# Fused block attention and FFN: second chunk's keys from a tile already loaded, later weight loads, later summaries and values

## The chip, the cores and the metric

One core of a Trainium2 chip. The metric is the device time of one execution in microseconds; the median of three runs of the kernel before is 690.5 us (688.78 to 691.71).

## The reference

Four batches, 8 heads, 768 positions, 64 elements per head. Each position attends to the positions less than 16 away and to 24 block summaries of its head, one for each block of 32 positions (the maximum of the block's keys, the mean of its values). The attention output, 3072 tokens of 512, goes through a feed-forward part:

```
scores_l = scale * q @ k^T                      # masked to |i - j| < 16
scores_s = scale * q @ k_sum^T + log(32)        # k_sum: maximum of 32 keys
a        = softmax(concat(scores_l, scores_s))
x        = a @ concat(v, v_sum)                 # v_sum: mean of 32 values
h        = x @ w_in                             # 512 -> 2048
out      = (h * tanh(softplus(h))) @ w_out      # 2048 -> 512
```

The weights arrive as 64-bit floats and are turned into float32 on the chip.

## The kernel before

The tokens are cut into 12 chunks of 256 (3 per batch). A unit is one chunk and one pair of heads; there are 48, and each is worked in phases:

- `att_scores` (L273): 16 matmuls of a 64-query tile against 96 keys and the 24 summaries (L284), or, for chunk 0, 32 matmuls with keys and summaries apart (L288, L290). DVE adds the mask and takes the row extreme (L299), ACT the exponentials (L304).
- `att_normalize` (L309): reciprocals on DVE (L313, L314), the product on POOL (L315).
- `att_transpose` (L317): four PE transposes (L321), one ACT copy to `pt` (L323).
- `att_values` (L326): 16 matmuls (L339), an ACT cast to `xh` (L340), and, by the returned function, the remainder `xl` on DVE (L341).

Two chunks make a group of 512 tokens, on which the feed-forward part (FFN below) runs in 16 steps, one for each block of 128 of the 2048: `ff_in` (12 matmuls, L353), Mish on ACT (L360), a split into two parts (L369, L371), and two steps later `ff_out` (12 matmuls, L381).

**Weights.** `load_weight` (L114) issues 1 MB as two DMAs (L119) into one of two buffers, `begin_weight` (L136) and `join_weight` (L149) make the float32 (ACT L143, DVE L144, L145, L154, L156), `upper_weight` (ACT, L129) and `lower_weight` (DVE, L134) split it. A load waits for the join of the load two before it. The one buffer of `f` makes L143 wait for the L134 before it.

**Order.** Under `tc.manual_schedule()` (L401) each engine runs its instructions in the order written; SP issues all DMAs, one after another, and a DMA that has to wait holds up those behind it. Before the FFN come ten turns u (L416); turn u holds the scores of unit u (u < 8), the values of unit u - 2 and the transposition of unit u - 1. Units 0 to 3 are chunk 0: their keys (`ks`, 768 positions), queries and values are loaded at the start by `first_keys` (L201) and `first_values` (L210), and their value summaries are 16 matmuls (L230, in two halves of 8), an ACT copy (L233) and a DMA from that into the values' tile (L234) in `first_value_summary`. Units 4 to 7 are chunk 1; `att_load_keys` (L244) loads queries and keys in one DMA of 496 KB (L251) and has POOL copy in the key summaries (L252). `att_load_values` (L255) loads `vw` (L258) and copies in the summaries (L259).

The FFN loop (L449) runs over steps i of all six groups; `at` (L396) says in which step which later unit has its scores: steps 0, 2, 4, 6, 8, 10, 12 and 13 in the first group. Transpositions come at the end of the next step, values in step i + 2. In even steps `att_load_keys` also loads `vsum` (L199) for a new batch, in odd ones `att_summaries` reduces it (L240, L241), moves it (L242) and loads the next keys (L195).

**PSUM.** Pool `ps_w` has four buffers, taken in turn by `ph` of `ff_in`, the two tiles of a unit's scores and, in the FFN loop, by `pt_ps` and `x_ps`.

Of the kernel before, what the change touches and what calls it, by code (L numbers as in the profile page):

```python
# [9 lines left out]
F32 = mybir.dt.float32  # L10
# [7 lines left out]
B, H, S, D = 4, 8, 768, 64  # L18
DM, DFF = 512, 2048
BLK, WIN = 32, 16  # L20
P = 128
NB = S // BLK
QT = 64
# [33 lines left out]
def fused_kernel(ctx: ExitStack, tc: tile.TileContext, q0, qk, kt, v0, vw, vs, w_in, w_out, out):  # L57
# [56 lines left out]
    def load_weight():  # L114
        if weights:
            w, fc = weights.pop(0)
            t = stage.tile([P, WB, WP], I64, tag="stage", name=f"w{w}_{fc}")
            for k in range(WB):
                nc.sync.dma_start(t[:, k, :], (w_in, w_out)[w][fc + k])  # L119
            loaded.append((w, fc, t))  # L120
# [28 lines left out]
    def join_weight():  # L149

        if begun:
            w, fc, f, x = begun.pop(0)
            u = f.bitcast(U32)
            nc.vector.tensor_scalar(out=f, in0=f, scalar1=-_as_f32(F32_MAX), scalar2=_as_f32(F32_MAX),  # L154
                                    op0=ALU.max, op1=ALU.min)
            nc.vector.scalar_tensor_tensor(out=u, in0=u, scalar=3, in1=x,  # L156
                                           op0=ALU.logical_shift_left, op1=ALU.bitwise_or)
            joined.append((w, fc, f))
            load_weight()


    begin = ExitStack()
# [23 lines left out]
    summary = {}  # L186
    xs = {}
    units = {}


    sources = {}

    def load_key_source(b, hp):
        ks = sources[b, hp, 0] = stage.tile([P, S], F32, tag="sum", name=f"ks{b}_{hp}", bufs=1)
        nc.sync.dma_start(ks, kt[b, hp])  # L195
# [5 lines left out]
    def first_keys(hp):  # L201

        ks = first_att.tile([P, WIN + S], F32, tag="ks", name=f"ks0_{hp}")
        nc.gpsimd.memset(ks[:, 0:WIN], 0.0)
        nc.sync.dma_start(ks[:, WIN:], kt[0, hp])
        t = first_att.tile([P, CH], F32, tag="q0", name=f"q0_{hp}")
        nc.sync.dma_start(t, q0[hp])
        units[0, hp] = {"q": t, "k": ks}

    def first_values(hp):  # L210
        vwt = first_att.tile([KA, NQ, P], F32, tag="vw", name=f"vw0_{hp}")
        nc.sync.dma_start(vwt[0:KW], vw[0, hp].rearrange("p (s k) -> p s k", s=NQ))
        t = first_att.tile([P, NR, P], F32, tag="v0", name=f"v0_{hp}", bufs=HP)
        nc.sync.dma_start(t, v0[hp].rearrange("p (j d) -> p j d", d=P))
        units[0, hp].update(v=vwt, rest=t)

    def key_summary(b, hp, keys):

# [4 lines left out]
    def first_value_summary(hp):  # L223

        vm = att.tile([KA, P], F32, tag="vm", name=f"vm0_{hp}", bufs=HP)[KW:KA]
        summary[0, hp].append(vm)
        vwt, t = units[0, hp]["v"], units[0, hp]["rest"]
        ps = att_psum(0, f"vm_ps0_{hp}")
        for j in range(NQ + NR):
            nc.tensor.matmul(ps[KW:KA, 0:P], *((blocks[0:KW, j, :], vwt[0:KW, j, :]) if j < NQ else  # L230
                                               (blocks[:, j, :], t[:, j - NQ, :])),
                             start=(j == 0), stop=(j == NQ + NR - 1))
        nc.scalar.copy(vm, ps[KW:KA, 0:P])  # L233
        nc.sync.dma_start(vwt[KW:KA], vm.unsqueeze(1).broadcast_to([NB, NQ, P]))  # L234
# [20 lines left out]
    def att_load_values(c, hp):  # L255
        b = c // CPB
        vwt = att.tile([KA, NQ, P], F32, tag="vw", name=f"vw{c}_{hp}")
        nc.sync.dma_start(vwt[0:KW], vw[c, hp].rearrange("p (s k) -> p s k", s=NQ))  # L258
        nc.sync.dma_start(vwt[KW:KA], summary[b, hp][1].unsqueeze(1).broadcast_to([NB, NQ, P]))  # L259
        units[c, hp]["v"] = vwt  # L260
# [12 lines left out]
    def att_scores(c, hp):  # L273
        u = units[c, hp]
        th = c % CPB


        ps = [att_psum(c, f"sc{c}_{hp}_{h}", scores=True) for h in range(2)]
        for s in range(NQ):
            for h in range(2):  # L280
                r = slice(h * D, (h + 1) * D)
                row, at0 = slice(s % 2 * QT, (s % 2 + 1) * QT), s // 2 * KA
                if c > 0:
                    nc.tensor.matmul(ps[h][row, at0:at0 + KA], u["qk"][r, s, h * QT:(h + 1) * QT],  # L284
                                     u["qk"][r, s, P:], start=True, stop=True)
                    continue
                q = u["q"][r, s * QT:(s + 1) * QT]
                nc.tensor.matmul(ps[h][row, at0:at0 + KW], q, u["k"][r, s * QT:s * QT + KW],  # L288
                                 start=True, stop=True)
                nc.tensor.matmul(ps[h][row, at0 + KW:at0 + KA], q, summary[0, hp][0][r, :],  # L290
                                 start=True, stop=True)
        pr = (att if c else first_att).tile([P, NQ, KA], F32, tag="pr", name=f"pr{c}_{hp}")


        nm = small.tile([P, NQ], F32, tag="nm", name=f"nm{c}_{hp}")
        for j in range(NQ):
            h, pair = divmod(j, NQ // 2)
            m = first if th == 0 and pair == 0 else last if th == CPB - 1 and pair == NQ // 2 - 1 else base
            nc.vector.tensor_tensor_reduce(  # L299
                out=pr[:, j, :], in0=ps[h][:, pair * KA:(pair + 1) * KA], in1=m, scale=-SCALE,  # L300
                scalar=-NEG, op0=ALU.add, op1=ALU.min, accum_out=nm[:, j:j + 1])
        sm = small.tile([P, NQ], F32, tag="sm", name=f"sm{c}_{hp}")
        for s in range(NQ):
            nc.scalar.activation(pr[:, s, :], pr[:, s, :], AF.Exp, scale=-1.0, bias=nm[:, s:s + 1],  # L304
                                 accum_out=sm[:, s:s + 1])
        u["p"] = pr
        u["sm"] = sm
# [9 lines left out]
    def att_transpose(c, hp):  # L317
        u = units[c, hp]
        ps = att_psum(c, f"pt_ps{c}_{hp}")
        for s in range(NQ):  # L320
            nc.tensor.transpose(ps[:KA, s * P:(s + 1) * P], u["p"][:, s, :], ident)  # L321
        pt = att.tile([KA, NQ, P], F32, tag="pt", name=f"pt{c}_{hp}", bufs=1)
        nc.scalar.copy(pt.rearrange("p s q -> p (s q)"), ps[:KA, :])  # L323
        u["pt"] = pt
# [91 lines left out]
    for u in range(n + 2):  # L416
        if u % 2 == 0:
            upper_weight()
        if u < n:
            att_scores(*todo[u])  # L420
        if u < HP:
            first_value_summary(u)
        lower = att_values(*todo[u - 2]) if 2 <= u else None
        if u % 2:
            join_weight()
        else:
            lower_weight()
            begin_weight()
        if u + 1 < HP:
            key_summary(0, u + 1, units[todo[u + 1]]["k"][:, WIN:])  # L430
        if lower:
            lower()
        if u == HP + 1:
            begin.close()
            late += weight_tiles(ctx.enter_context(tc.tile_pool(name="late", bufs=1)), "w_late", NFC - EARLY)
        if u < n:
            att_normalize(*todo[u])
        if HP - 2 <= u < n:
            att_load_keys(*todo[u + 2])
        if HP <= u:  # L440
            att_load_values(*todo[u])
        if 1 <= u <= n:
            att_transpose(*todo[u - 1])

    load_key_source(1, 0)
    waiting = []
    for i in range(len(steps) + 2):  # L449
        upper_weight()  # L450
        if i < len(steps):
            ff_in(*steps[i])
            ff_act(*steps[i])
            if i < NFC:
                waiting.append(ff_split(*steps[i]))
        if 0 < i <= NFC:
            waiting.pop(0)()
        lower_weight()
        lower = att_values(*at[i - 2]) if i - 2 in at else None
        if lower and i >= NFC:  # L460
            lower()
        if i in at:
            att_scores(*at[i])
        begin_weight()
        if lower and i < NFC:
            lower()
        if NFC <= i < len(steps):
            ff_split(*steps[i])()
        if i in at:
            att_normalize(*at[i])  # L470
        join_weight()
        if i in at:
            if todo.index(at[i]) + 2 < len(todo):
                att_load_keys(*todo[todo.index(at[i]) + 2])
        if i - 2 in at and todo.index(at[i - 2]) + 2 < len(todo):
            att_load_values(*todo[todo.index(at[i - 2]) + 2])
        if i - 1 in at:
            att_summaries(todo.index(at[i - 1]) + 2)
        if i >= 2:
            ff_out(*steps[i - 2])  # L480
        if i - 1 in at:
            att_transpose(*at[i - 1])
# [44 lines left out]
```

## Time and profile before

| what | value |
|---|---|
| median of three runs | 690.5 us |
| profiled execution | 691.24 us, of which the span is 689.5 us |
| PE busy | 641.1 us (93%) |
| DVE busy | 290.6 us (42%) |
| ACT busy | 332.9 us (48%) |
| POOL busy | 68.1 us (10%) |
| moved by DMA | 71.05 MB |
| mean granted TensorE clock | 0.967 |

PE is the tensor engine's matmuls, DVE the vector engine, ACT the scalar engine, POOL GpSimd and SP the engine that issues DMAs. Shares over the whole span hide that its stretches differ: the turns before the FFN, the first FFN steps with weights still being prepared, and the rest. A bracket in a timeline row is the engine's idle time just before the instruction, with what released it.

### The profile page before, as it was taken

What the parts mean: (1) busy time and instruction counts of PE and PEld (TensorE: products, weight loads), DVE (VectorE), ACT (ScalarE), POOL (GpSimd) and SP (SyncE); (2) the same over time, 40 slices, a digit from 0 to 9 for tenths busy, and PEclk for the clock granted to TensorE, in tenths of its full rate; (3) what the DMA queues carried; (4) which work ended last, traced back from release to release, by engine and by line L of the source; (5) the groups of instructions that cost most, each with busy time, mean ns of one, the idle gap of its engine ahead of it and who ended that gap; (6) DMA issues with size and microseconds to landing.
All of it is one profiled execution on the core that took longest, in us unless ns stands there. A gap on an engine that the chain in (4) does not pass through costs nothing.

```text
span 689.5 us, 10881 instructions
## 1 busy us (share of the span) xinstructions
PE 641.1 (93%) x4160; PEld 513.9 (75%) x4160; DVE 290.6 (42%) x836; ACT 332.9 (48%) x722; POOL 68.1 (10%) x119
## 2 busy tenths in 40 slices
PE   4845798879999999999999999999999999999997
PEld 3634576667778878878878878878788788888886
DVE  3866889895223225453232244442242232221112
ACT  2655776668555445454554554454464454111111
POOL 3121011021101001001001001001001000000000
PEclk9866899999999999999999999999999999999999
DMA  8776455744232122542112134432141110010001
GB/s 281 197 259 217 153 190 212 213 152 141 59 106 87 45 67 92 158 153 89 45 48 85 44 130 114 134 113 68 45 140 54 45 59 0 1 62 0 1 1 61
DMA packets 31253, 71.05 MB, mean 103 GB/s; under 512 B 4833, under 2 KB 9953, under 8 KB 31201
## 3 DMA queue, kind: packets, MB, share of 16 engines
q1 hardware_dynamic: 31200, 70.35, 31.9%
q8 instruction: 33, 0.54, 0.3%
q14 instruction: 20, 0.16, 0.1%
HBM read 61.54 MB, written 6.29 MB: 98 GB/s over the span
## 4 chain that ended last, share of the span: by engine, by line
PE 79%; DMA 6%; ACT 6%; DVE 5%; issue 2%; SPq 1%; POOL 0%; POOLq 0%; ACTq 0%; DVEq 0%
PE po L381 35%; PE ph L353 34%; PE x_ps L339 4%; PE sc L284 3%; PE pt_ps L321 3%; DVE w_f L156 2%; DMA vsum<-vs 2%; DMA q<-q 1%; DMA v<-v 1%; DVE w_f L154 1%; ACT w_f L143 1%; DMA qk<-qk 1%; ACT pr L304 1%; DMA vw<-vm 1%; ACT L360 1%
## 5 line engine op out<-in xcount | busy, mean ns | idle before, releaser
L360 ACT ACTIVATE a<-ph 128x512 f32<-128x512 f32 x96 | 57.4, 598 | 155.4 <-PE ph L353 155.0
L369 DVE CAST ah<-a 128x512 fp32r<-128x512 f32 x80 | 34.0, 425 | 197.1 <-ACT a L360 197.1
L353 PE MATMUL ph<-xh,w_early_in_hi 128*128 128x512 f32 x240 | 97.8, 407 | 0.0
L381 PE MATMUL po<-w_early_out_hi,ah 128*128 128x512 f32 x240 | 97.5, 406 | 0.0
L360 ACT ACT_TABLE_LOAD x41 | 52.6, 1283 | 88.6 <-PE ph L353 88.4
L353 PE MATMUL ph<-xh,w_early_in_lo 128*128 128x512 f32 x240 | 94.9, 396 | 0.0
L353 PE MATMUL ph<-xl,w_early_in_hi 128*128 128x512 f32 x240 | 94.8, 395 | 0.0
L381 PE MATMUL po<-w_early_out_lo,ah 128*128 128x512 f32 x240 | 94.3, 393 | 0.0
L381 PE MATMUL po<-w_early_out_hi,al 128*128 128x512 f32 x240 | 94.1, 392 | 0.0
L315 POOL TENSOR_TENSOR pr<-pr,rs 128x480 f32<-128x480 f32 x48 | 49.2, 1026 | 394.9 <-DVE rs L314 327.5
L304 ACT ACTIVATE pr<-pr,nm 128x120 f32<-128x120 f32 x192 | 73.5, 384 | 16.8 <-DVE nm L299 16.3
L341 DVE TENSOR_TENSOR xl<-x_ps,xh 128x256 fp32r<-128x256 f32 x48 | 20.3, 423 | 119.8 <-ACT xh L340 119.8
L371 DVE TENSOR_TENSOR al<-a,ah 128x512 fp32r<-128x512 f32 x96 | 66.3, 691 | 2.8
L381 PE MATMUL po<-w_late_out_hi,ah 128*128 128x512 f32 x144 | 58.0, 403 | 0.0
L353 PE MATMUL ph<-xh,w_late_in_hi 128*128 128x512 f32 x144 | 57.6, 400 | 0.0
L381 PE MATMUL po<-w_late_out_lo,ah 128*128 128x512 f32 x144 | 56.3, 391 | 0.0
L353 PE MATMUL ph<-xh,w_late_in_lo 128*128 128x512 f32 x144 | 56.2, 391 | 0.0
L353 PE MATMUL ph<-xl,w_late_in_hi 128*128 128x512 f32 x144 | 56.1, 390 | 0.0
L381 PE MATMUL po<-w_late_out_hi,al 128*128 128x512 f32 x144 | 56.0, 389 | 0.0
L381 PEld LDWEIGHTS po<-w_early_out_hi,ah 128*128 128x128 f32 x240 | 45.7, 190 | 13.1 <-issue 4.4
L339 PEld LDWEIGHTS x_ps<-pt,vw 120*64 120x64 f32 x768 | 29.0, 149 | 33.5 <-issue 18.5
L353 PEld LDWEIGHTS ph<-xh,w_early_in_lo 128*128 128x128 f32 x240 | 45.8, 191 | 10.2
(74 smaller groups left out, 934.5 us busy)
## 6 DMA issues: line engine op xcount, KB each, us to landing
qk<-qk SPq DMA_DIRECT2D x44, 496.0 KB
vw<-vw SPq DMA_DIRECT2D x48, 192.0 KB
w<-w_in SPq DMA_DIRECT2D x16, 512.0 KB
w<-w_out SPq DMA_DIRECT2D x16, 512.0 KB
ks<-kt SPq DMA_DIRECT2D x17, 384.0 KB
out<-o SPq DMA_DIRECT2D x24, 256.0 KB
vsum<-vs SPq DMA_DIRECT2D x12, 384.0 KB
vw<-vm SPq DMA_DIRECT2D x48, 48.0 KB
```

Source lines behind the costliest of these rows:

```text
L156: nc.vector.scalar_tensor_tensor(out=u, in0=u, scalar=3, in1=x, op0=ALU.logical_shift_left, op1=ALU.bitwise_or)
L284: nc.tensor.matmul(ps[h][row, at0:at0 + KA], u["qk"][r, s, h * QT:(h + 1) * QT], u["qk"][r, s, P:], start=True, stop=True)
L304: nc.scalar.activation(pr[:, s, :], pr[:, s, :], AF.Exp, scale=-1.0, bias=nm[:, s:s + 1], accum_out=sm[:, s:s + 1])
L315: nc.gpsimd.tensor_mul(pr, pr, rs.unsqueeze(2).broadcast_to([P, NQ, KA]))
L321: nc.tensor.transpose(ps[:KA, s * P:(s + 1) * P], u["p"][:, s, :], ident)
L339: nc.tensor.matmul(x, u["v"][:, s, d], pt, start=True, stop=True)
L341: return lambda: nc.vector.tensor_sub(xl, ps[:, :CH], xh.bitcast(F32))
L353: nc.tensor.matmul(ph, w[:, cc * P:(cc + 1) * P], x[:, cc, :], start=(cc == 0 and n == 0), stop=(cc == NCC - 1 and n == 2))
L360: nc.scalar.activation(a, st[g, fc], AF.Mish)
L369: (nc.scalar.copy if g == 0 else nc.vector.tensor_copy)(ah, a)
L371: return lambda: nc.vector.tensor_sub(al, a, ah.bitcast(F32))
L381: nc.tensor.matmul(po[g][t], a[:, tok], w, start=(fc == 0 and n == 0), stop=(fc == NFC - 1 and n == 2))
```

## The change

Five edits. Chunk 1 takes its keys from `ks`, shifted by 256 positions, and its scores are the 32 matmuls of chunk 0; the queries' tile is twice as wide, and `more_queries` fills the second half with two DMAs per unit in turns 2 to 5, from the part of `qk` that holds queries (4 runs of 64 floats in each of 64 partitions per DMA). The tile of values `v0` is kept in `rests`. The pool of the first turns is closed in turn 7, not 5. The weights' load is the last thing in an odd turn, and in an FFN step comes after the loads of keys, values and summaries. The value summaries of units 0 to 3 come behind the transposition. The values of units whose scores are in steps 0 to 10 come three steps later, not two.

```diff
--- before.py
+++ after.py
@@ -156,7 +156,6 @@
             nc.vector.scalar_tensor_tensor(out=u, in0=u, scalar=3, in1=x,
                                            op0=ALU.logical_shift_left, op1=ALU.bitwise_or)
             joined.append((w, fc, f))
-            load_weight()
 
 
     begin = ExitStack()
@@ -186,6 +185,7 @@
     summary = {}
     xs = {}
     units = {}
+    rests = {}
 
 
     sources = {}
@@ -203,16 +203,25 @@
         ks = first_att.tile([P, WIN + S], F32, tag="ks", name=f"ks0_{hp}")
         nc.gpsimd.memset(ks[:, 0:WIN], 0.0)
         nc.sync.dma_start(ks[:, WIN:], kt[0, hp])
-        t = first_att.tile([P, CH], F32, tag="q0", name=f"q0_{hp}")
-        nc.sync.dma_start(t, q0[hp])
-        units[0, hp] = {"q": t, "k": ks}
+        t = first_att.tile([P, CG * CH], F32, tag="q0", name=f"q0_{hp}")
+        nc.sync.dma_start(t[:, :CH], q0[hp])
+        for c in range(CG):
+            units[c, hp] = {"q": t[:, c * CH:(c + 1) * CH], "k": ks[:, c * CH:]}
+
+    def more_queries(hp):
+
+        t, other = units[1, hp]["q"], qk[1, hp].rearrange("p (s k) -> p s k", s=NQ)
+        for h in range(2):
+            r = slice(h * D, (h + 1) * D)
+            nc.sync.dma_start(t[r].rearrange("p (s k) -> p s k", s=NQ), other[r, :, h * QT:(h + 1) * QT])
 
     def first_values(hp):
         vwt = first_att.tile([KA, NQ, P], F32, tag="vw", name=f"vw0_{hp}")
         nc.sync.dma_start(vwt[0:KW], vw[0, hp].rearrange("p (s k) -> p s k", s=NQ))
         t = first_att.tile([P, NR, P], F32, tag="v0", name=f"v0_{hp}", bufs=HP)
         nc.sync.dma_start(t, v0[hp].rearrange("p (j d) -> p j d", d=P))
-        units[0, hp].update(v=vwt, rest=t)
+        units[0, hp].update(v=vwt)
+        rests[hp] = t
 
     def key_summary(b, hp, keys):
 
@@ -224,7 +233,7 @@
 
         vm = att.tile([KA, P], F32, tag="vm", name=f"vm0_{hp}", bufs=HP)[KW:KA]
         summary[0, hp].append(vm)
-        vwt, t = units[0, hp]["v"], units[0, hp]["rest"]
+        vwt, t = units[0, hp]["v"], rests.pop(hp)
         ps = att_psum(0, f"vm_ps0_{hp}")
         for j in range(NQ + NR):
             nc.tensor.matmul(ps[KW:KA, 0:P], *((blocks[0:KW, j, :], vwt[0:KW, j, :]) if j < NQ else
@@ -280,7 +289,7 @@
             for h in range(2):
                 r = slice(h * D, (h + 1) * D)
                 row, at0 = slice(s % 2 * QT, (s % 2 + 1) * QT), s // 2 * KA
-                if c > 0:
+                if c >= CG:
                     nc.tensor.matmul(ps[h][row, at0:at0 + KA], u["qk"][r, s, h * QT:(h + 1) * QT],
                                      u["qk"][r, s, P:], start=True, stop=True)
                     continue
@@ -418,8 +427,6 @@
             upper_weight()
         if u < n:
             att_scores(*todo[u])
-        if u < HP:
-            first_value_summary(u)
         lower = att_values(*todo[u - 2]) if 2 <= u else None
         if u % 2:
             join_weight()
@@ -430,20 +437,27 @@
             key_summary(0, u + 1, units[todo[u + 1]]["k"][:, WIN:])
         if lower:
             lower()
-        if u == HP + 1:
+        if u == n - 1:
             begin.close()
             late += weight_tiles(ctx.enter_context(tc.tile_pool(name="late", bufs=1)), "w_late", NFC - EARLY)
         if u < n:
             att_normalize(*todo[u])
-        if HP - 2 <= u < n:
+        if HP - 2 <= u < n - 2:
+            more_queries(u + 2 - HP)
+        if n - 2 <= u < n:
             att_load_keys(*todo[u + 2])
         if HP <= u:
             att_load_values(*todo[u])
         if 1 <= u <= n:
             att_transpose(*todo[u - 1])
-
-
-
+        if u < HP:
+            first_value_summary(u)
+        if u % 2:
+            load_weight()
+
+
+
+    values = {i + (3 if i < NFC - 4 else 2): unit for i, unit in at.items()}
     load_key_source(1, 0)
     waiting = []
     for i in range(len(steps) + 2):
@@ -456,7 +470,7 @@
         if 0 < i <= NFC:
             waiting.pop(0)()
         lower_weight()
-        lower = att_values(*at[i - 2]) if i - 2 in at else None
+        lower = att_values(*values[i]) if i in values else None
         if lower and i >= NFC:
             lower()
         if i in at:
@@ -472,10 +486,11 @@
         if i in at:
             if todo.index(at[i]) + 2 < len(todo):
                 att_load_keys(*todo[todo.index(at[i]) + 2])
-        if i - 2 in at and todo.index(at[i - 2]) + 2 < len(todo):
-            att_load_values(*todo[todo.index(at[i - 2]) + 2])
+        if i in values and todo.index(values[i]) + 2 < len(todo):
+            att_load_values(*todo[todo.index(values[i]) + 2])
         if i - 1 in at:
             att_summaries(todo.index(at[i - 1]) + 2)
+        load_weight()
         if i >= 2:
             ff_out(*steps[i - 2])
         if i - 1 in at:
```

## Rows read from the trace of the kernel before

**Rows 1.** Three stretches: length, busy us of each engine (instructions), PEclk, DMA share, GB/s.

```profile
0.00:62.00 62.00, 32.73 (x416) 24.93 (x416) 39.20 (x115) 30.66 (x93) 14.62 (x41) 0.79 0.75 239
62.00:160.00 98.00, 82.66 (x482) 64.87 (x481) 81.42 (x143) 69.17 (x121) 10.81 (x11) 0.91 0.56 186
160.00:689.50 529.50, 525.67 (x3268) 424.08 (x3268) 169.99 (x578) 233.09 (x509) 42.69 (x67) 1.00 0.23 72
```

**Rows 2.** Waits of PE, whole span: us in total, times, longest us.

```profile
PE x_ps L339 <- ACT pt L323: 11.6, 8, 2.8
PE sc L284 <- POOL qk L252: 9.1, 2, 4.7
```

**Rows 3.** Chain that ended last, before the FFN: start us, us, what.

```profile
52.28 1.24 DVE w_f L156
...
55.38 5.57 DMA vw<-vm
```

**Rows 4.** Timeline of PE, the last unit of values before the FFN: start us, us.

```profile
61.08 1.12 PE L339 MATMUL x_ps<-pt,vw 120*64 120x64 f32 x16 [5.09 <-DMA vw<-vm]
```

**Rows 5.** Timeline of DVE, turns 4 to 7.

```profile
32.12 0.28 DVE L299 CUSTOM_DVE_ANT_0 pr<-sc,base 128x120 f32<-128x120 f32 x1
...
36.69 0.18 DVE L314 RECIPROCAL rs<-rs 128x4 f32<-128x4 f32 x1
39.45 0.28 DVE L299 CUSTOM_DVE_ANT_0 pr<-sc,base 128x120 f32<-128x120 f32 x1 [2.59 <-PE sc L284]
...
42.78 0.28 DVE L299 CUSTOM_DVE_ANT_0 pr<-sc,base 128x120 f32<-128x120 f32 x1
...
50.74 0.28 DVE L299 CUSTOM_DVE_ANT_0 pr<-sc,base 128x120 f32<-128x120 f32 x1 [3.21 <-PE sc L284]
```

**Rows 6.** Timeline of PE, turns 2 to 4.

```profile
22.65 1.90 PE L230 MATMUL vm_ps<-v,blocks 128*24 128x128 f32 x8 [0.70 <-DMA v<-v]
24.48 1.12 PE L339 MATMUL x_ps<-pt,vw 120*64 120x64 f32 x16
...
26.57 0.62 PE L288 MATMUL sc<-ks,q 64*64 64x96 f32 x8
...
27.82 1.61 PE L230 MATMUL vm_ps<-vw,blocks 96*24 96x128 f32 x8
...
30.23 0.69 PE L339 MATMUL x_ps<-pt,vw 120*64 120x64 f32 x16
...
31.43 0.64 PE L284 MATMUL sc<-qk 64*64 64x120 f32 x16
```

**Rows 7.** DMA packets by size, from 21 to 22 us, then from 58 to 59 us.

```profile
DMA packets 230, 0.25 MB, mean 246 GB/s; under 512 B 30, under 2 KB 154, under 8 KB 230
...
DMA packets 112, 0.43 MB, mean 431 GB/s; under 512 B 3, under 2 KB 3, under 8 KB 112
```

**Rows 8.** Timeline of ACT, turn 8: copy of the last unit's transposed probabilities.

```profile
57.48 0.58 ACT L323 COPY pt<-pt_ps 120x512 f32<-120x512 f32 x1
```

**Rows 9.** Timeline of DVE, FFN steps 7 to 11.

```profile
123.02 1.21 DVE L134 TENSOR_TENSOR w_late_out_lo<-w_f,w_late_out_hi 128x1024 fp32r<-128x1024 f32 x1
...
130.94 1.22 DVE L240 TENSOR_REDUCE vq<-vsum 96x32 f32<-96x1024 f32 x1 [2.61 <-DMA vsum<-vs]
...
141.29 1.21 DVE L134 TENSOR_TENSOR w_late_out_lo<-w_f,w_late_out_hi 128x1024 fp32r<-128x1024 f32 x1
...
157.12 1.21 DVE L134 TENSOR_TENSOR w_late_out_lo<-w_f,w_late_out_hi 128x1024 fp32r<-128x1024 f32 x1
```

**Rows 10.** Timeline of ACT, FFN steps 11 and 12.

```profile
158.76 0.62 ACT L369 CAST ah<-a 128x512 fp32r<-128x512 f32 x1
...
160.93 0.37 ACT L340 CAST xh<-x_ps 128x256 fp32r<-128x256 f32 x1
```

**Rows 11.** Timeline of PE, values in FFN steps 6 and 12.

```profile
111.05 1.12 PE L339 MATMUL x_ps<-pt,vw 120*64 120x64 f32 x16 [2.67 <-ACT pt L323]
...
159.92 0.69 PE L339 MATMUL x_ps<-pt,vw 120*64 120x64 f32 x16 [0.47 <-ACT pt L323]
```

## The prediction

> **What bounds the kernel now.** I read the windows first, because the page's share of 93% for PE hides three different stretches [rows 1]. From 160 us on PE is busy 525.67 of 529.5 us at the full granted clock (2.4 GHz): the change touches nothing there that it could shorten. Before 62 us, in the ten turns, PE is busy 32.73 us of 62 and DVE 39.20: here something else is awaited. From 62 to 160 us PE is busy 82.66 of 98 and DVE 81.42. So only the first 160 us can gain.
>
> Then the waits of PE [rows 2]. In the turns it waited 9.1 us in two waits for the POOL copy that follows the 496 KB load of chunk 1; the wait for `pt` before values, 11.6 us in eight, belongs nearly all to the FFN steps.
>
> Then the chain before the FFN [rows 3]: the DVE join that ends at 53.52, the load of a weight that SP had held for that join, and behind it the DMA of the summaries, issued at 55.38 and 5.57 us on the way. The values of unit 7 started at 61.08 after waiting 5.09 for it [rows 4], and the FFN follows them at once. So SP's order, a load that waits for DVE ahead of small DMAs that PE needs, sets the start of the FFN.
>
> Last, DVE in turns 4 to 7 [rows 5]: the mask instruction of a turn follows the reciprocal of the turn before with no gap in turn 6 (42.78), but after 2.59 us in turn 5 and 3.21 in turn 7, both waits for scores. The reader is to see that, without the qk load, the turns run at DVE's pace.
>
> **The change, part by part.** I call T4 and T7 the start of the mask on DVE in turns 4 and 7.
>
> *Keys from the tile.* This removes four qk loads and four POOL copies. DVE's own work in an even turn is 36.69 + 0.18 - 32.12 = 4.75 us, in an odd one 42.78 - 39.45 = 3.33 [rows 5]. So T7 = T4 + 4.75 + 3.33 + 4.75 = T4 + 12.83, where it was 18.62. The sixteen more matmuls in each of four units cost PE some 0.3 us a unit, from 31.43 on 0.64 for sixteen, and 1.25 for thirty-two at the low clock, 26.57 to 27.82 [rows 6]; in turns at DVE's pace DVE's weight work covers that; if the cover went, it would be 1.2 us in all.
>
> *Summaries behind transpositions.* PE now does, in turn 2, values(0), transposition(1), the summary of unit 2, and only then scores(3). Values(0) need the summary's DMA, which before was hidden: they ran at 24.48 with no wait [rows 6]. It is a DMA of 96 pieces of 512 B behind the first loads; in the 21 to 22 us window 154 pieces under 2 KB moved [rows 7], about the time of the two summary DMAs under way (192 pieces). I take 22.3. Then values and transposition 26.57 - 24.48 = 2.1, the two summary halves 2 x 1.83 (22.65 to 24.48, at the low clock, which I expect after the wait), scores(3) 1.25: that makes 29.3. In turn 3 values and transposition 31.43 - 30.23 = 1.2, the summary 30.23 - 27.82 = 2.41, scores(4) 0.95, between 0.64 and 1.25: T4 = 33.9 where it was 32.12. This part alone loses 1.8 us. Bounds: without any wait DVE's pace would put T4 at 30.9 (an estimate: 1.2 before 32.12, since the 1.83 of the summary no longer stands ahead); with the DMA landing at 24.48, its latest, T4 is 36.0.
>
> *Weights' loads last in a turn.* SP now issues `vw` and the summary copy of turn 7 ahead of the load that waits for DVE. The 5.09 us wait goes, and next in line is `pt`: ACT's copy ended at 57.48 + 0.58 = 58.06 [rows 8], 7.32 after T7 = 50.74. So values(7) start at T7 + 7.32. The load itself is delayed by three or four small DMAs, at most by a wait for values or for the reduction of `vsum`; it has two turns or two steps (15.83 us, below) until it is begun, so I cost that at nothing; if that cover is gone, DVE waits at L144 and each late us is a us of its loop.
>
> Head together: T7 = 33.9 + 12.83 = 46.7, values(7) at 54.0 instead of 61.08: 7.1 us less; from the bounds 10.1 and 5.0.
>
> *The FFN steps to 160 us.* DVE prepares a weight in each step and this loop, with ACT's part in it, sets the pace: from L134 to L134 two steps later it took 157.12 - 141.29 = 15.83 us [rows 9], while PE has only 82.66 of 98 us to do. Values one step later shift `xh` and `xl` from even to odd steps; the pair of steps holds the same work, so the loop does not get shorter by it. The two DMAs of `att_load_values` move with them, on SP's queue from even to odd steps, ahead of L242 and L195; their readers come a step later too, but for the last two units of the group, which keep two steps (15.83 us) for a transfer that took 5.57 at the worst seen here [rows 3]: nothing. What does shorten it: the pair before took 141.29 - 123.02 = 18.27, with a wait of 2.61 for `vsum`, which had been issued behind a weight's load. Now it stands ahead of it: 18.27 - 15.83 = 2.4 us less. Zero if `vsum` is late for another reason.
>
> Where does the removed wait for `pt`, 11.6 us, go? Not off the time: PE will wait elsewhere for the same loop. In `ps_w` the second scores tile of an even step now takes the buffer that `x_ps` of the step before leaves, so scores wait for `xl`. At the loop's end this matters: in step 11 ACT's cast begins at 158.76 and takes 0.62, then `xh` 0.37 [rows 10] and `xl`, which I put at the same (an estimate): 160.1. Before, values ran at 159.92 and took 0.62 or so [rows 11], so scores came at 160.54. Now scores come at 160.1 but those values are still to be done: 0.2 lost. And PE had waited some 2.4 us there: the same sixteen matmuls took 1.12 after a wait of 2.67 and 0.69 after one of 0.47 [rows 11], the granted clock being 0.91 over the stretch [rows 1]. That is 18% of 98 us at 1.2 GHz, 8.8 us of work lost in about six resumptions (an estimate), 1.5 each. Behind those scores stand `ff_out` of step 10 and all of PE's later work. I take 1.0 of the 0 to 1.5, because 2.4 lies nearer to 2.67. Together: -2.4 + 0.2 + 1.0 = -1.2.
>
> *Free edits.* Closing the pool in turn 7 touches tiles first written in step 6. POOL has idle time for all it does (14.62 of 62 us, [rows 1]). The four queries' pairs of DMAs: below.
>
> Sum: 691.24 - 7.1 - 1.2 = 682.9 for a profiled execution. The profiled one lay 0.7 above the median of 690.5, so **682.2**.
>
> *A row and a rule.* `more_queries` moves 512 pieces of 256 B a unit where qk moved 128 large ones. In the window with 154 small pieces 230 packets passed in a us, in the other 112 large ones [rows 7]: 512 pieces are 2.2 us by the first rate, 1.1 if the 76 others took 76/112 of that us; qk took 1.15. By 2.2, the third unit's queries, issued behind a 1 MB load at about 34 us, land near 40 us, when scores(6) want them (T4 + 6.7): the sum holds by either. The Trainium skill (DMA: Bandwidth & Descriptors, "Specifications") asks for transfers of at least 512 B for full rate; no row here shows 256 B pieces in bulk. It gives a rival.
>
> **Rivals.**
> 1. *The summary is there in time.* T4 = 30.9, and PE resumes at the full clock: -10.1 - 2.4 + 0.2 makes 678.2 at the median. For it: PE waited nowhere for that DMA in turns 2 to 4. Against: small pieces still moved from 21 to 22 us.
> 2. *The queries come late.* If a 256 B piece costs twice the 512 B one, a unit takes 4.4 us; the third unit's land near 42.3, the fourth's near 47.3, behind `vw`, where T7 wants them a us before 46.7: T7 moves by 2.5 to 49.2, and the time is 684.7. For it: SP issues them between the loads. Against: DMA is busy only 0.75 of the stretch [rows 1]. By the rule of the Trainium skill named above this is the case to expect.
> 3. *The turns gain little.* Summary at 24.48, and `vsum` late all the same: -5.0 + 1.2 + 0.2 is 686.9, within 0.5% of the time before with any late query; this is also the case that the change does not do what it says. For it: DVE has 39.2 us of work in the turns whatever is removed.
> 4. *Slower: the PSUM buffer.* `xl` of an odd step comes behind L134, L144 and L145, some 3.5 us after the step's L134, and scores need 1.1 more; DVE wants them about 9 us after that L134 (half of 15.83, and L134 itself). So there are 4.5 us of slack. If values come later than that, each pair grows by the excess; it decides at 2.4 us excess in each of five pairs, 12 us, which gives 694.2. For it: the ring is really shared so. Against: the slack.
>
> **Chances.** Forecast 0.49 (own range 679 to 685.5), rival 1 0.25, rival 2 0.13, rival 3 0.09, rival 4 0.04. The range reaches from a little under rival 1 to the far end of rival 3: 676.5 to 687.5. Half a per cent, 3.5 us, is about what a measurement of this kernel can tell from no change; 687.0 is that bound. Forecast and rivals 1 and 2, less 0.03 for their ends: faster 0.84. Rival 3 and that rest: same 0.12. Rival 4: slower 0.04.
>
> **What would show it.** Right: no wait of PE for the POOL copy in the turns, T7 near T4 + 12.8, values(7) started by ACT's `pt` at about 54 us, scores(3) later than before; no DVE wait for `vsum` of over 1 us before 160 us; waits of PE for `pt` replaced by waits of scores for DVE's `xl`; nothing changed in length after the first FFN group. Wrong: a wait of scores(6) or (7) for a DMA of queries, DVE waiting at L144 for a load, or FFN pairs of steps that are clearly longer or shorter than 15.8 us.

## The result, and the profile of the changed kernel

The changed kernel takes **683.12 us** at the median of four runs (681.82 to 684.43), the kernel before 690.31 in the same comparison (688.78 to 691.71): a ratio of 0.9896, 95% interval 0.9867 to 0.9926. Faster by 1.0%; the prediction was 682.2 us, range 676.5 to 687.5. The profiled execution took 684.43 us with a span of 682.7, where 691.24 and 689.5 stood before. The total is right, but the experiments show that I had credited the wrong edit with most of it.

The three stretches of the changed kernel, columns as in [rows 1]:

```profile
0.00:62.00 62.00, 39.37 (x491) 31.17 (x492) 40.84 (x117) 33.96 (x96) 13.91 (x37) 0.78 0.76 225
62.00:160.00 98.00, 86.44 (x523) 66.01 (x521) 84.01 (x155) 72.11 (x130) 12.08 (x14) 0.95 0.56 189
160.00:682.70 522.70, 518.99 (x3218) 418.81 (x3214) 166.32 (x564) 227.60 (x497) 40.30 (x64) 1.00 0.22 71
```

PE is busy 6.64 us more before 62 us (39.37 for 32.73) and 3.78 more in the next 98; the stretch after that, at the full clock as before, is 6.8 us shorter (522.70 for 529.50). Now PE's waits, whole span, columns as in [rows 2]:

```profile
PE sc L293 <- ACT pt L332: 6.5, 5, 2.0
...
PE x_ps L348 <- ACT pt L332: 4.9, 4, 1.9
...
PE x_ps L348 <- DMA vw<-vm: 3.3, 1, 3.3
PE sc L293 <- ACT a L369: 2.3, 3, 1.4
PE sc L297 <- DMA q<-qk: 1.2, 1, 1.2
```

The 9.1 us for POOL's copy behind qk are gone, and so are the values' waits for `pt` in the FFN steps (the four that are left lie in the turns). New are one wait of 3.3 us for a summary's DMA, one of 1.2 for queries, and waits of scores in the FFN steps. The timeline of PE shows the first two of these and the end of the turns:

```profile
24.42 1.12 PE L348 MATMUL x_ps<-pt,vw 120*64 120x64 f32 x16 [3.34 <-DMA vw<-vm]
26.51 1.90 PE L239 MATMUL vm_ps<-vw,blocks 96*24 96x128 f32 x8
...
42.72 0.75 PE L297 MATMUL sc<-ks,q 64*64 64x96 f32 x4 [1.21 <-DMA q<-qk]
...
56.63 1.12 PE L348 MATMUL x_ps<-pt,vw 120*64 120x64 f32 x16 [1.65 <-ACT pt L332]
```

Unit 7's values start at 56.63 instead of 61.08 [rows 4], held by ACT's copy and no longer by a DMA. DVE's masks of turns 4, 6 and 7, to be set beside [rows 5]:

```profile
35.05 0.28 DVE L308 CUSTOM_DVE_ANT_0 pr<-sc,base 128x120 f32<-128x120 f32 x1 [0.36 <-PE sc L299]
...
44.46 0.28 DVE L308 CUSTOM_DVE_ANT_0 pr<-sc,base 128x120 f32<-128x120 f32 x1 [1.32 <-PE sc L299]
...
48.93 0.28 DVE L308 CUSTOM_DVE_ANT_0 pr<-sc,base 128x120 f32<-128x120 f32 x1
```

T4, 32.12 before, is 35.05, later by 2.9; T7, 50.74 before, is 48.93. And the chain of the turns (start us, us, what) names the two DMAs that stand in it:

```profile
16.81 7.47 DMA vw<-vm
24.42 1.12 PE x_ps L348 x16
...
36.52 6.07 DMA q<-qk
42.72 0.91 PE sc L297 x6
```

The last L134 of the loop, which the prediction measured at 157.12 [rows 9], now starts here:

```profile
150.18 1.22 DVE L134 TENSOR_TENSOR w_late_out_lo<-w_f,w_late_out_hi 128x1024 fp32r<-128x1024 f32 x1
```

From that L134 to the end of the span it is 532.5 us, and 532.4 before: everything was won ahead of it.

### The profile page after: what moved, and what is told of

Same layout as the page of the kernel before. It is cut to its first block, busy times and chain, and to the rows that moved or that the text cites. A ratio compares the mean times of both kernels' runs of the same rounds, so it can differ in the third digit from the quotient of the medians.

```text
span 682.7 us, 11000 instructions
## 1 busy us (share of the span) xinstructions
PE 644.8 (94%) x4224; PEld 516.0 (76%) x4224; DVE 291.2 (43%) x836; ACT 333.7 (49%) x722; POOL 66.3 (10%) x115
## 4 chain that ended last, share of the span: by engine, by line
PE 80%; ACT 9%; DVE 5%; DMA 3%; issue 1%; SPq 0%
PE po L390 36%; PE ph L362 34%; PE x_ps L348 4%; PE sc L293 3%; PE pt_ps L330 2%; DVE w_f L156 2%; ACT w_f L143 2%; DVE w_f L154 2%; ACT pr L313 1%; PE vm_ps L239 1%; ACT L369 1%; ACT L313 1%; DMA vw<-vw 1%; DMA vw<-vm 1%; ACT a L369 1%
## 5 line engine op out<-in xcount | busy, mean ns | idle before, releaser
L390 PEld LDWEIGHTS po<-w_early_out_lo,ah 128*128 128x128 f32 x240 | 45.9, 191 | 10.3
```

The lines of the kernel that those rows point to most:

```text
L390: nc.tensor.matmul(po[g][t], a[:, tok], w, start=(fc == 0 and n == 0), stop=(fc == NFC - 1 and n == 2))
```

## The experiments

Each kernel is the changed one with one part undone, unless said otherwise. I cut every profiled execution at the same marks: T4 and T7 (the masks of turns 4 and 7), v7 (the start of unit 7's values), L (the start of the L134 that was at 157.12). The runs were made on three chips (e1 to e4, e5 to e8, e9 to e12), each beside the kernel before (medians 690.19, 689.6, 689.54), so that kernels are compared by their ratio to it, and 0.001 of the ratio is 0.7 us.

| kernel | T4 | T7 - T4 | v7 - T7 | L - v7 | span - L | median us | ratio to before, 95% interval |
|---|---|---|---|---|---|---|---|
| before | 32.12 | 18.62 | 10.34 | 96.04 | 532.4 | 690.31 | 1 |
| changed | 35.05 | 13.88 | 7.70 | 93.55 | 532.5 | 683.12 | 0.9896 (0.9867 to 0.9926) |
| e1 summary back | 30.38 | 13.06 | 7.63 | 94.05 | 534.2 | 681.04 | 0.9855 (0.9828 to 0.9883) |
| e2 queries early | 34.53 | 12.73 | 7.60 | 93.76 | 532.6 | 683.11 | 0.9899 (0.9877 to 0.9921) |
| e3 both of these | 29.91 | 12.79 | 7.62 | 92.94 | 532.5 | 679.0 | 0.9854 (0.9828 to 0.9881) |
| e4 values back | 34.26 | 13.19 | 7.65 | 93.11 | 533.9 | 684.13 | 0.9909 (0.9889 to 0.9929) |
| e5 turns' loads back | 32.94 | 17.91 | 10.51 | 93.11 | 532.5 | 690.73 | 1.0013 (0.9993 to 1.0032) |
| e6 steps' loads back | 32.88 | 13.97 | 7.65 | 93.16 | 532.5 | 683.14 | 0.9907 (0.9885 to 0.9929) |
| e7 keys back | 33.73 | 14.36 | 7.63 | 93.12 | 532.7 | 683.36 | 0.9914 (0.9891 to 0.9937) |
| e8 query rows | 31.97 | 12.91 | 7.67 | 93.22 | 532.7 | 681.54 | 0.9889 (0.9867 to 0.9910) |
| e9 before, turns' loads last | 30.02 | 15.06 | 7.62 | 95.26 | 532.3 | 682.57 | 0.9901 (0.9881 to 0.9922) |
| e10 both steps' edits back | 33.26 | 13.43 | 7.65 | 93.56 | 532.3 | 682.66 | 0.9906 (0.9882 to 0.9930) |
| e11 e3 with e8 | 32.01 | 12.79 | 7.61 | 93.04 | 532.7 | 679.97 | 0.9861 (0.9838 to 0.9885) |
| e12 before, again | 30.29 | 18.54 | 10.40 | 94.95 | 532.4 | 688.28 (one run) | |

**e1, the summary ahead of the values again.**

```diff
             att_scores(*todo[u])
+        if u < HP:
+            first_value_summary(u)
         lower = att_values(*todo[u - 2]) if 2 <= u else None
...
             att_transpose(*todo[u - 1])
-        if u < HP:
-            first_value_summary(u)
```

> The changed kernel with the value summaries of units 0 to 3 back in their old place, ahead of values and transposition. Theory: in the changed kernel PE waits 3.34 us for the summary's DMA in turn 2 and the summary of unit 2 then stands between that wait and scores(3); with the old place the mask of turn 4 on DVE, at 35.05 in the changed kernel, comes back to about 32.4 us, and the median falls from 683.1 to about 680.5. Rival: the queries of unit 6 land at the same 42.6 us anyway, since they stand behind a weight's load on the queue; then turn 6 is not earlier, and the median stays within 0.7 us of 683.1.

v7 falls from 56.63 to 51.07, 5.6 us earlier. Of that the profiled execution keeps 3.4 (681.04 us against 684.43), and the ratio 0.0041, some 2.8 us: in the profile the loop takes 0.5, and 1.7 go behind L, where the granted clock drops in this execution. Its windows, columns as in [rows 1]:

```profile
145.00:150.00 5.00, 3.59 (x27) 2.42 (x26) 3.37 (x6) 4.91 (x8) 0.34 (x1) 0.94 0.78 233
150.00:155.00 5.00, 5.00 (x17) 3.95 (x16) 2.11 (x12) 3.50 (x10) 2.02 (x3) 0.71 0.34 104
```

The edit to the summaries is a loss, although the intervals of e1 and of the changed kernel overlap: the three kernels with the keys from the tile, the loads last and the summary ahead (e1, e3, e11) have ratios of 0.9854 to 0.9861, the seven that differ from them by the summary behind (the changed kernel, e2, e4, e6, e7, e8, e10, some with one more part undone) 0.9889 to 0.9914. The whole table bears on its size: with the summary behind (the changed kernel, e2, e4 to e8, e10) T4 lies from 31.97 to 35.05, mean 33.6; with it ahead (before, e1, e3, e9, e11, e12) from 29.91 to 32.12, mean 30.8. That is 2.8 us.

**e2, all queries issued in turn 2**, and **e3, e1 and e2 together.**

```diff
-        if HP - 2 <= u < n - 2:
-            more_queries(u + 2 - HP)
+        if u == HP - 2:
+            for hp in range(HP):
+                more_queries(hp)
```

> The changed kernel with all eight DMAs of the second chunk's queries issued in turn 2, ahead of the summary's DMA that SP waits with and ahead of two weights' loads. Theory: the wait of PE for queries in turn 6 (1.21 us) goes, DVE's gap of 1.32 us before the mask of turn 6 with it, the start of turn 4 stays at about 35.0, and the median falls by 1.0 to 1.3, to about 682.0. Rival: the wait was only one of several that end together (the transposition of turn 5 ended 41.5); then the gap shrinks by less than 0.4 us and nothing is gained.

> Both edits of the two runs before together. Theory: the two waits are one behind the other on the way to the FFN, so their gains add: turn 4 at about 32.4, values of unit 7 at about 52.7 instead of 56.6, median about 679.2. Rival: once PE is earlier the turns are bound by DVE's weight work and the join's data, and the gain is that of the summary alone, 680.5.

In e2 PE's wait for queries and DVE's gap in turn 6 are gone, T7 - T4 is 12.73, and v7 is 1.8 earlier; the ratio is that of the changed kernel (0.9899, 0.9896), and the 1.0 to 1.3 us that I expected did not come. So 1.8 us of one profile against another is within what executions of one kernel differ by (before: 688.31 to 692.42 in these runs), and the gain is not shown. e3 is the fastest kernel of the study at 679.0, but its interval is nearly that of e1.

**e4, values two steps after their scores again.**

```diff
-    values = {i + (3 if i < NFC - 4 else 2): unit for i, unit in at.items()}
+    values = {i + 2: unit for i, unit in at.items()}
```

> The changed kernel with the values of all later units two steps after their scores, as before the change. Theory: the later values gained nothing, because scores of even steps now wait for the same ACT copy of transposed probabilities (6.5 us in five waits) that values waited for before, and DVE's weight loop sets the pace; the median stays within 0.7 us of 683.1, the lower-weight instruction of step 11 within 0.5 us of 150.2. Rival: the later values are worth what the old wait was, 1 to 2.7 us a pair of steps, and the median rises to 685 or more.

L - v7 does not grow (93.11). The waits change places again, as PE's waits from 62 us on show (the scores have none), here in e4 and then in the kernel before:

```profile
PE x_ps L348 <- ACT pt L332: 11.9, 6, 2.8
...
PE x_ps L339 <- ACT pt L323: 10.6, 6, 2.8
```

So values wait in the steps as they did before the change, where in the changed kernel scores wait 6.5 and 2.3 us. Behind L the profiled execution loses 1.4 us, where the last of these waits, of 1.81 us, is followed by scores that take 1.02 us instead of 0.64, in a window whose granted clock is 0.67. The median, 684.13, is inside the scatter. The edit moves waits and is worth nothing that can be measured.

**e5, the weights' load inside the turn again, as it was before; all other edits kept.**

```diff
             join_weight()
+            load_weight()
         else:
...
-        if u % 2:
-            load_weight()
```

> The changed kernel with the weight's load of the odd turns back directly behind the join, ahead of queries, values and summaries on SP; the FFN steps stay as changed. Theory: SP again holds the queries of unit 7 and the values and summary of units 5 and 7 until DVE's join, and 1 MB goes ahead of them: scores(7) wait about 1.5 us and values(7) about 1.5 to 2 us for a DMA; median about 686. Rival: with the 496 KB loads gone the transfers are short enough, and the order of the loads is worth under 0.7 us.

This decides the study: 690.73 us, a ratio of 1.0013, where I had expected 686. With this one edit undone nothing of the gain is left, although qk is not loaded in the turns that waited for it. PE's waits from 14 to 62 us:

```profile
PE x_ps L348 <- DMA vw<-vm: 7.7, 2, 4.7
PE sc L297 <- DMA q<-qk: 6.9, 3, 3.6
```

Scores wait 6.9 us for 128 KB of queries as they waited 9.1 for 496 KB [rows 2]. How long SP held the weight's load for DVE's join (L156) from 28 to 56 us stands in its own waits, of the kernel before, of e5 and of the changed kernel:

```profile
SPq L119 <- DVE w_f L156: 14.1, 2, 7.4
...
SPq L119 <- DVE w_f L156: 10.3, 2, 5.2
...
SPq L119 <- DVE w_f L156: 1.4, 1, 1.4
```

SP's queue in e5 shows what stood behind the load (start us, us, engine, line), and PE's timeline who waited for it:

```profile
36.93 0.87 SPq L268 DMA_DIRECT2D vw<-vm  x1
42.95 0.81 SPq L119 DMA_DIRECT2D w<-w_in  x2
43.81 1.21 SPq L216 DMA_DIRECT2D q<-qk  x2
...
53.78 0.82 SPq L119 DMA_DIRECT2D w<-w_out  x2
...
55.59 0.83 SPq L268 DMA_DIRECT2D vw<-vm  x1
```

```profile
48.93 0.55 PE L297 MATMUL sc<-ks,q 64*64 64x96 f32 x2 [3.12 <-DMA q<-qk]
...
61.36 1.12 PE L348 MATMUL x_ps<-pt,vw 120*64 120x64 f32 x16 [4.69 <-DMA vw<-vm]
```

The 14.1 us are 7.4 ahead of turn 7's qk and 6.7 ahead of unit 7's summaries. In e5, from 37.8 to 42.95, SP issues nothing: the load waits for DVE's join. The queries of turn 7 leave at 43.81, behind that and behind 1 MB; PE does their scores from 48.93, after a wait of 3.12. The summaries of unit 7 leave at 55.59, behind the next weight's load at 53.78, and values(7) start at 61.36 after 4.69. The size of what stands behind the waiting load counts for less than its place: 6.9 against 9.1 us. The Trainium skill (DMA: Bandwidth & Descriptors, "Anatomy of one DMA — SWDGE (gpsimd) path", a section on DMAs that GpSimd issues) says that DMA engines do not wait on semaphores and that the issuing sequencer does so before it dispatches; this trace, of DMAs that SP issues, agrees, with 5.2 us in which SP issues nothing.

**e6, the loads of the FFN steps ahead again.**

```diff
-        join_weight()
+        if begun:
+            join_weight()
+            load_weight()
...
-        load_weight()
```

> The changed kernel with the weight's load of the FFN steps back directly behind the join, ahead of the source of the value sums, keys and values. Theory: DVE again waits over 2 us for that source in step 7, the weight loop is longer by 2.4 us, and the median rises to about 685.5. Rival: the long wait of the kernel before came from its own timing; no DVE wait for the source above 1 us, median within 0.7 us of 683.1.

The ratio is 0.9907 where the changed kernel has 0.9896, well inside the intervals, and DVE waits nowhere for `vsum` before 160 us. The 2.61 us wait of [rows 9], on which my term of -2.4 stood, does not come back with its supposed cause.

**e7, chunk 1's keys from qk again.**

```diff
-        for c in range(CG):
-            units[c, hp] = {"q": t[:, c * CH:(c + 1) * CH], "k": ks[:, c * CH:]}
+        units[0, hp] = {"q": t[:, :CH], "k": ks}
...
-                if c >= CG:
+                if c > 0:
...
-        if HP - 2 <= u < n - 2:
-            more_queries(u + 2 - HP)
-        if n - 2 <= u < n:
+        if HP - 2 <= u < n:
             att_load_keys(*todo[u + 2])
```

> The changed kernel with chunk 1 again loading queries and keys in one DMA of 496 KB per unit, with the POOL copy of the summaries, and sixteen matmuls; all other edits stay. Theory: the load for units 6 and 7 waits for a buffer until scores(4) and (5) are done and then takes 3.5 us or more, so that PE again waits for the POOL copy in turns 6 and 7, some 4 us in all; median about 687. Rival: the order of loads alone did it, and without weights ahead the 496 KB arrive in time; median within 1 us of 683.1.

683.36 us, where I had expected 687: with the 496 KB loads back, nothing measurable is lost (a ratio of 0.9914, inside the interval of the changed kernel). PE's waits from 14 to 62 us:

```profile
PE sc L292 <- POOL qk L260: 2.5, 3, 1.6
```

With the weights' load out of their way the qk loads cost 2.5 us of waits instead of 9.1, and T7 - T4 is 14.36, 0.5 more than in the changed kernel and 1.2 more than the mean of its kin (the nine kernels with the keys from the tile and the turns' loads last: 12.73 to 13.97, mean 13.2). So the edit to which I gave 5.8 us of T7 - T4 is worth about 1 in profiles and nothing that can be measured in the time, with the summary behind. (With the summary ahead it may be worth more: see e9.)

**e8, queries in rows of 1 KB**, from an array of 512 positions laid out so before the launch, one DMA for each unit instead of two. Nothing is left out of the computation.

```diff
...
-        t, other = units[1, hp]["q"], qk[1, hp].rearrange("p (s k) -> p s k", s=NQ)
-        for h in range(2):
-            r = slice(h * D, (h + 1) * D)
-            nc.sync.dma_start(t[r].rearrange("p (s k) -> p s k", s=NQ), other[r, :, h * QT:(h + 1) * QT])
+        nc.sync.dma_start(units[1, hp]["q"], q0[hp][:, CH:])
...
```

> The changed kernel with the second chunk's queries taken from an array that holds 512 positions in a row, one DMA per unit with 128 pieces of 1 KB instead of two with 512 pieces of 256 B; same places in SP's order, same bytes. Theory: the small pieces are cheap (377 of them passed in a microsecond with the DMA engines half busy), the wait of scores(6) comes from the weight's load ahead, and the median stays within 0.7 us of 683.1, perhaps 0.3 lower by SP's shorter issue. Rival: the small pieces make the queries late; the wait of 1.21 us goes and the median falls by 1.0 or more.

1.6 us less at the median and 0.5 by the ratio (0.9889 against 0.9896), inside the interval of the changed kernel: inconclusive between theory and rival. No wait for queries is left, but SP's part is shorter too (0.43 to 0.52 us in place of 1.20), so this kernel cannot tell the pieces' size from the issuing time.

**e9, the kernel before with the load last in the odd turns, and nothing else.**

```diff
             joined.append((w, fc, f))
-            load_weight()
...
             att_transpose(*todo[u - 1])
+        if u % 2:
+            load_weight()
...
-        join_weight()
+        if begun:
+            join_weight()
+            load_weight()
```

> The kernel before with one edit: the weight's load of the odd turns issued last in the turn. Keys, summaries, values and the FFN steps' loads stay as before. Theory after the first eight runs: this place in SP's order is what the change gained in the turns, so values(7) start at 54 to 57 us with no wait for a summary's DMA above 1 us, and the median is 681 to 684; without the later summaries, which cost some 2 us, nearer 681. Rival: the order helps only with the small queries in place of 496 KB; waits for the POOL copy stay at 5 us or more and the median is 687 or more.

682.57 us, a ratio of 0.9901 (0.9881 to 0.9922): this one edit wins as much as the whole change. T7 - T4 is 15.06, with the qk loads and POOL's copies all there. PE's waits for these copies from 14 to 62 us, and SP's for the join from 28 to 56 us:

```profile
PE sc L283 <- POOL qk L251: 4.4, 3, 2.5
...
SPq L119 <- DVE w_f L156: 2.2, 2, 1.2
```

SP waits 2.2 us for the join instead of 14.1, since the load now comes late in the turn, nearer the end of the join. v7 is at 52.70, 3.9 earlier than in the changed kernel: T4, with the summary ahead, is 5.0 earlier, and T7 - T4 is 1.2 longer. The equal total is not an equal sum, though. Against e1, e3 and e11, which also have the summary ahead, e9 loses 2.0 to 2.3 us of T7 - T4 and 1.2 to 2.3 in the loop, and its ratio is 0.0040 to 0.0047 higher, about 3 us. They differ from it by the keys from the tile and by the edits to the FFN steps. Since undoing the latter costs nothing in e10, where the summary is behind, the keys are probably worth some of this once it is ahead; no run here undoes them alone in such a kernel, so that is not shown. The loop is longer than the changed kernel's by 1.7 and shows a wait like that of [rows 9]:

```profile
121.74 1.22 DVE L239 TENSOR_REDUCE vq<-vsum 96x32 f32<-96x1024 f32 x1 [2.13 <-DMA vsum<-vs]
```

**e10, both edits to the FFN steps undone** (the diffs of e4 and e6 together).

> The changed kernel with both edits of the FFN steps undone: values two steps after their scores, loads directly behind the join. Theory: each was undone alone with a stretch of 93.1 us from values(7) to the lower-weight of step 11 (96.0 before, 93.6 after), so neither made it shorter: the stretch is 93 to 94 again, with at most the loss of clock seen with the values back (1.4 us behind step 12); median 683 to 685. Rival: either edit alone is enough to keep the source of the value sums in time, and with neither DVE waits for it again over 2 us: stretch 95.5 to 96, median 685.5 or more.

682.66 us, L - v7 93.56, and 0.35 us of wait for `vsum` in step 7. The two edits together are worth nothing measurable here.

**e11, the summary ahead, queries early and in rows** (the diffs of e1, e2 and e8 together).

> A version meant to be faster: loads last in turns, summaries in their old place, the second chunk's queries as rows of 1 KB in one DMA per unit, all four issued in turn 2; FFN steps as changed. Theory: turns are at DVE's pace (turn 4 at about 30, turn 7 at 42.7), so the median is that of the two edits without the rows, 679.0, within 1 us. Rival: shorter issues on SP let the values' DMAs of units 4 and 5 start earlier and take their waits (2.4 us in two) away: 677.5 or less.

679.97 us with a ratio of 0.9861: e3 again, so that the rows add nothing once the queries are early. e1, e3 and e11 lie together (0.9854 to 0.9861), by these ratios 2.4 to 2.9 us under the changed kernel; each of their intervals still overlaps its own.

**e12, the kernel before, profiled once more.**

> The kernel before, unchanged, for another profile. Theory: the wait of 2.61 us of DVE for the source of the value sums in step 7 was of that one execution (the DMA engines moved 205 to 303 GB/s there where 400 are seen elsewhere): here no such wait above 1 us in steps 0 to 10, and 93 to 94.5 us from values(7) to the lower-weight of step 11. Rival: it belongs to the kernel, and stands there again with 2 us or more and 95.5 to 96.5 us.

T4 is 30.29 where it was 32.12, and the wait for `vsum` in step 7 is 1.23 us instead of 2.61. T7 - T4 (18.54) and v7 - T7 (10.40) agree with the first to 0.1. The loop, 94.95 where it was 96.04, lies between what my theory (up to 94.5) and its rival (from 95.5) had said. In this one pair of executions, then, the columns T7 - T4 and v7 - T7 repeat, while T4, that wait and the loop differ by 1 to 2 us.

## Why the prediction was right, and where it was not

- **"Keys from the tile" is the step that failed.** It put all of T7's shortening, from T4 + 18.62 to T4 + 12.83, on the removed qk loads. Undone alone (e7) they cost 0.5 us of it, and e9 against e1, e3 and e11, with the summary ahead, 2.0 to 2.3 at most; the loads' order undone alone (e5) costs 4.0. I read the 9.1 us wait for POOL's copy as the price of a large transfer; it was mostly the price of a place in SP's queue (with the load behind them these waits are 4.4 us in e9 and 2.5 in e7). The reading of [rows 3], that SP's order sets the start of the FFN, was right, and I applied it to the last turn only: such a load stood ahead of the qk of turns 5 and 7 as well, in the kernel before:

```profile
31.52 0.94 SPq L119 DMA_DIRECT2D w<-w_out  x2
32.51 0.93 SPq L251 DMA_DIRECT2D qk<-qk  x2
...
42.29 0.81 SPq L119 DMA_DIRECT2D w<-w_in  x2
43.27 0.33 SPq L251 DMA_DIRECT2D qk<-qk  x1
```

Ahead of turn 7's the load waited 7.4 us for the join. Ahead of turn 5's SP waited for DVE by 0.4 us only, so there it was the place behind a megabyte, or behind the summary's DMA issued at 30.62, and which of the two is not shown. In e9 the qk of turn 5 leaves at 29.50, ahead of the load, and PE waits 2.50 us for its copy instead of 4.33.

- **"Weights' loads last in a turn"** was right in mechanism: the wait for the summaries goes, ACT's `pt` is next. v7 is T7 + 7.70, and T7 + 7.60 to 7.67 in the other ten with the load last; I had 7.32. It also holds 4.7 us of the turns (17.91 in e5 against the mean of 13.2), which I had credited elsewhere: with 10.51 less 7.65 that is 7.6 us, and e5's ratio is 0.0117 above the changed kernel's, some 8 us.
- **"Summaries behind transpositions"** had the right sign and too small a size: 1.8 taken, 2.9 in the profile and 2.8 over fourteen executions. The term that was off is the summary's landing. I took 22.3 us from the packets in flight; it was issued at 16.81, took 7.47 and landed at 24.28, near the bound of 24.48. T4, put at 33.9 with a bound of 36.0, came at 35.05.
- **Rival 2, the late queries,** came true in place and not in size. The third unit's queries, issued behind a weight's load, landed at 42.59 (36.52 + 6.07), where I had said 42.3, and DVE lost 1.32 us in turn 6, not 2.5 in turn 7. Its cause, the price of the pieces, is not shown (below).
- **The head together:** 4.45 us were won to v7 where 7.1 were forecast and 5.0 was the far bound. The summary's landing, the queries and 0.4 of the last turn make up the 2.6 that are missing.
- **"The FFN steps to 160 us":** -2.49 in the loop where I had -2.4, but not shown to come from the order of the loads: e6, e4 and e10 undo what was to cause it, singly and together, and their loops are 93.1 to 93.6. The three kernels whose loop is longer (before 96.04, e12 94.95, e9 95.26) have qk loads in the turns, the summary ahead and the old steps, all at once, and each waits for `vsum` in step 7. Which of these brings that wait stays open; it was not tried singly in such a kernel. The two executions of the kernel before differ by 1.1 here, so against the second only 1.4 of the 2.49 is left.
- **Waits in the steps:** I expected scores to wait for `xl` on DVE. By the trace they waited for ACT, 6.5 us for `pt` copies and 2.3 for Mish. The loop's length, which I had said would set the time, did not feel it.
- **The +1.0 for the clock** (and 0.2 for the displaced values) was not paid in the changed kernel, 532.5 us behind L against 532.4; e1 paid 1.7 and e4 1.4.

So a head that came out 2.65 us too long was met by a loop with its clock that was 1.2 us better than forecast: 684.43 us profiled instead of 682.9, and a median 0.9 off. That it lies so near is luck, by offsetting errors, and not a right account.

## What to carry to other kernels

A DMA that must wait for a compute engine is best put last among those that its queue issues in that stage: its wait (5.2 us ahead of the queries of turn 7 in e5), and whatever its megabyte adds, which no run here separates, are paid by every transfer behind it that an engine needs soon, and the wait shows under the name of the small one's consumer. When several edits touch one wait, undo each alone before crediting any: here one edit alone won as much as the whole bundle, another in the bundle gave away 2 to 3 us, and what a third is worth seems to depend on the second. Putting work that waits for a DMA ahead of work that waits for nothing turns a hidden transfer into a wait of the engine.

## What the runs showed that I had not expected

**What small pieces cost depends on the window.** Packets of the changed kernel from 33 to 34 us, nearly all of them queries, and the window of the same stretch (columns as in [rows 1]):

```profile
DMA packets 377, 0.09 MB, mean 89 GB/s; under 512 B 377, under 2 KB 377, under 8 KB 377
```

```profile
33.00:34.00 1.00, 1.00 (x11) 0.94 (x10) 1.00 (x2) 0.98 (x4) 0.00 (x0) 1.00 0.47 89
```

377 packets of some 256 B passed in a us with the DMA engines 0.47 busy. The 512 of a unit would then be 0.64 us of all engines (512 / 377 x 0.47), where I had 1.1 to 2.2. In bytes that is 189 GB/s for fully busy engines (89 / 0.47, an estimate), under half of the 431 GB/s of large packets in [rows 7]. The Trainium skill's rule that transfers want 512 B for full rate (DMA: Bandwidth & Descriptors, "Specifications") agrees with that, but at 128 KB a unit the loss of rate in this window is under half a us. From 40 to 41 us, when the late queries of unit 6 were on the way together with others, it looks different:

```profile
DMA packets 507, 0.25 MB, mean 251 GB/s; under 512 B 448, under 2 KB 448, under 8 KB 507
```

```profile
40.00:41.00 1.00, 0.24 (x2) 0.24 (x3) 1.00 (x5) 1.00 (x7) 0.71 (x1) 1.00 1.22 251
```

Here the engines are full (share 1.22). If the 59 large packets, some 0.14 MB, went at 431 GB/s, they took 0.3 us, and the 448 small ones 0.9, which is 1.0 us for 512 (an estimate): near the lower end of what I had put, and far from rival 2's 4.4.

**The clock does not answer to a wait alone.** Scores of step 12 had the same last wait in the changed kernel and in e1 (0.99 us for `pt`). In the changed kernel the windows of that wait and after it are at the full clock, and in e1 the next is the one at 0.71 shown above, part of it at 1.2 GHz, though PE was as busy in the window of the wait (3.58 us, and 3.59 in e1):

```profile
150.00:155.00 5.00, 3.58 (x28) 2.44 (x27) 3.41 (x6) 4.91 (x8) 0.21 (x1) 1.00 0.74 233
155.00:160.00 5.00, 5.00 (x37) 3.94 (x35) 2.14 (x12) 3.98 (x11) 2.05 (x3) 1.00 0.37 104
```

So these rows do not tell which wait will cost clock: the price, 1.4 to 1.7 us of later work where it was paid (e4, e1), was paid in one execution and not in another with the same wait, and is better carried as a chance than as a term.
